# Output projection with norms out of place and stores as steps of their own, and the mixing stage's first rows beside the last attention unit

## The chip, the cores and the metric

The kernel runs on one core of one Trainium2 chip. The metric is device microseconds of one execution of the whole program. A core has five engines with an instruction queue each: TensorE (PE, with its weight loads shown as PEld), VectorE (DVE), ScalarE (ACT), GpSimd (POOL) and SyncE (SP). Here SP issues nearly all DMAs, one after the other; a DMA whose condition is not met holds everything behind it in SP's queue.

## The reference

```python
x = A_x                                               # 2048 x 576
sa, ca, ga, sb, cb, gb = silu(c) @ w_mod              # six vectors of 576
h = layernorm(x) * (1 + ca) + sa
x = x + ga * (sliding_attention(h @ wqkv) @ wo)       # 32 heads of 18, window 256
h = layernorm(x) * (1 + cb) + sb
g = gelu(layernorm(h) @ w1)                           # then four column groups shifted by +1, -1, +2, -2 rows
x1 = h + shifted(g) @ w2
x = x + gb * (x1 + gelu(layernorm(x1) @ w3) @ w4)     # w3: 576 x 4608
```

All matrix products work on operands split into a high and a low part (three products per chunk of 128), 14 matmuls for a contraction of 576.

## The kernel before

The program has three stages. `phase_a` is attention and most of the output projection, `phase_b` the mixing stage (w1, the shifts, w2), `phase_c` the large MLP. The order of instructions on every engine in `phase_a` is written out by hand: each step is a pair (time, function), the time in attention units, and `play` emits the functions by rising time. The times are a plan; on the chip each engine simply works through its queue. In `phase_b` the order is the framework's.

`phase_a` runs 32 units `u` (four blocks `g` of 512 rows by eight groups `j` of four heads). A unit lasts some 20 us. For unit `u`, `pack(u)` issues twelve DMAs from SP that gather the rows of q and k from DRAM into `Q[u % 3]` and `K[u % 3]`, planned at `u - 1.6`; they can start when the last read of that buffer, three units before, is done. `scores(u)` (planned from `u - 1` to `u`) takes row maxima, `attend(u)` (from `u + 0.38`) makes the exponentials on ACT (L549), the products with V (L560, 48 matmuls), and writes `o` to the DRAM tensor `od` (L581).

From unit 22.85 on, `s4a(t)` for the row tiles t = 0 to 11 runs beside the attention, one tile each 0.72 units: two rows are loaded (`or`, the attention output, and `xr`, the input; eight slots of `s4rows`, but tile 0 has rows of its own), `or` is transposed and multiplied with `Wo` (L786), the result added into `xr` (L791), `xr` stored to `xp` (L793), normed in place on ACT (L158), scaled and shifted in place on POOL (`mod`, L801 and L802), stored to `hbd` (L803), normed in place again (`ln2`, L158) and stored to `xnd` (L807). Each store stands right behind the instruction that makes its data. A norm in place writes the row that the store before it reads, so ACT waits until that store has landed.

The last four tiles (`s4`, t = 12 to 15) need the attention output of the last unit and run in `phase_b`, which begins with the first block's rows: `stage1(t)` loads `xn` rows from `xnd` (L984) and transposes them (L98, L104) into `xnT0`; `stage2(0)` multiplies that with five chunks of w1 (L1017) and applies the gelu (L1019, which needs another ACT table). `xnT` tiles come from a ring of three buffers.

Of the kernel before, what the change touches and what calls it, by code (L numbers as in the profile page):

```python
# [53 lines left out]
class Kern:  # L54
# [133 lines left out]

    def phase_a(self):
        nc = self.nc  # L190
        sm, gp, row = self.sm, self.gp, self.row
        self.hbd = [self.dr.tile([P, D], F32, name=f"hbd{t}") for t in range(NT)]
        self.xnd = [self.dr.tile([P, D], F32, name=f"xnd{t}") for t in range(NT)]
# [5 lines left out]
        with ExitStack() as st:  # L199
            ps = self.bank  # L200
            kv = self.pool(st, "kV")
            kp = self.pool(st, "kA")
            V = [kv.tile([P, H * VA + 13], F32, name=f"V{i}") for i in range(10)]
# [316 lines left out]
            def attend(u):  # L520
# [53 lines left out]
                def on():  # L574
                    pt = abox[2]
                    rc = sm.tile([P, 4, 4], F32, tag="rc", name=f"rc{u}", bufs=2)
                    nc.vector.reciprocal(rc, pt[:, :, :, DH])
                    o = kp.tile([P, 4, 72], F32, tag="o", name=f"o{u}", bufs=2)
                    nc.vector.tensor_tensor(out=o.rearrange("p t (h d) -> p t h d", d=DH), in0=pt[:, :, :, 0:DH], in1=rc.unsqueeze(3).to_broadcast([P, 4, 4, DH]), op=ALU.mult)
                    j = u % NU  # L580
                    nc.sync.dma_start(self.od[g].rearrange("(t p) d -> p t d", p=P)[:, :, j * 72:(j + 1) * 72], o)  # L581
                e = []
                for b in range(3):
# [2 lines left out]
                        e += [(t, xs(b, h)), (t + 0.015, ex(b, h))]  # L586
                    e.append((u + self.o_x + 1 + self.o_a - 0.001 * (2 - b), av(b)))
                t = u + self.o_x + 1 + self.o_a
                return e + [(t + 0.03, cp), (t + 0.15, ot), (t + 0.165, on)]

            def modvec(v):
                acc = []

                def load(k):
                    def f():
                        if k == 0:
                            acc.append(gp.tile([P, 2 * D], F32, tag="oT", name=f"wm{v}", bufs=1))
                            acc.extend((acc[0][:, 0:D], acc[0][:, D:]))
                        kk = P if k < KC else TAIL
                        nc.scalar.dma_start(acc[1 if k == 0 else 2][:kk], self.w_mod[k * P:k * P + kk, v * D:(v + 1) * D])  # L600
                    return f

                def add(k):
                    def f():
                        w = acc[1 if k == 0 else 2]
                        kk = P if k < KC else TAIL
                        nc.gpsimd.tensor_scalar(w[:kk], w[:kk], silu[:kk, k:k + 1], 0.0, op0=ALU.mult, op1=ALU.add)
                        if k:
                            nc.gpsimd.tensor_tensor(out=acc[1][:kk], in0=acc[1][:kk], in1=w[:kk], op=ALU.add)
                    return f  # L610

                def bcast(hf):
                    def f():
                        acc.append(ps([P, 288], "tr", f"pm{v}{hf}"))
                        nc.tensor.matmul(acc[-1], ones.to_broadcast([P, P]), acc[1][:, hf * 288:(hf + 1) * 288], start=True, stop=True)

                    def e():
                        nc.vector.tensor_scalar(acc[1][:, hf * 288:(hf + 1) * 288], acc[3 + hf], 1.0 if v == 4 else 0.0, None, op0=ALU.add)
                        if hf == 1:
                            nc.sync.dma_start(self.modd[v], acc[1][0:1, :])  # L620
                    return [(0.3, f), (0.33, e)]
# [103 lines left out]
            for t in range(12):  # L725
                t0 = w1 + 0.12 + 0.72 * t
                ev += [(t0 + d, f) for d, f in self.s4a(t, kp)]
            ev += self.load_w1(w1 + 1.2, 0.56) + self.load_w2(w1 + 4.1, 0.6)
            with self.tc.manual_schedule(engines={mybir.EngineType.SP, mybir.EngineType.PE, mybir.EngineType.DVE, mybir.EngineType.Activation, mybir.EngineType.Pool}):
                play(ev)  # L730

    win = {1: (2.9, 9.25), 2: (9.7, 16.1), 3: (16.55, 22.73)}
    o_p, o_x, o_a, g_w = 1.6, 0.38, 0.18, 0.05

    def s4a(self, t, kp):
# [39 lines left out]
        def wo(hf):  # L775
            cs = slice(hf * 288, (hf + 1) * 288)

            def part(a, b):
                def f():
                    T, W = box["T"], Wo["w"]  # L780
                    if a == 0:
                        box["po"] = ps([P, 288], "mm", f"po{t}_{hf}")
                    pl = sorted(self.products(lambda k: k, lambda k: k), key=lambda p: p[0] // KC)
                    pl = [(T[:, i, :], W[:, j, cs]) for i, j in pl]
                    for n in range(a, b):
                        nc.tensor.matmul(box["po"], pl[n][0], pl[n][1], start=(n == 0), stop=(n == len(pl) - 1))  # L786
                return f

            def add():
                x = box["x"]  # L790
                nc.vector.tensor_tensor(out=x[:, cs], in0=box["po"], in1=x[:, cs], op=ALU.add)  # L791
                if hf == 1:
                    nc.sync.dma_start(self.xp[t], x)  # L793
            return [part(a, b) for a, b in ((0, 4), (4, 8), (8, 11), (11, 14))], add

        x = lambda: box["x"]
        b1, r1, n1, g1 = self.stat_steps(x, f"b{t}")
        b2, r2, n2, g2 = self.stat_steps(x, f"c{t}")

        def mod():  # L800
            nc.gpsimd.tensor_tensor(out=x(), in0=x(), in1=self.cb, op=ALU.mult)  # L801
            nc.gpsimd.tensor_tensor(out=x(), in0=x(), in1=self.sb, op=ALU.add)  # L802
            nc.sync.dma_start(self.hbd[t], x())  # L803

        def ln2():
            self.norm(x(), x(), g2())
            nc.sync.dma_start(self.xnd[t], x())  # L807
# [141 lines left out]
    def ltile(self, name):  # L949
        if name == "LNT0":  # L950
            return self.gp.tile([P, 2 * KC + 1, 512], F32R, tag="L", name=name, bufs=1)
        return self.bc.tile([P, 2 * KC + 1, 512], F32R, tag="L2", name=name, bufs=3)

    def phase_b(self, bp):
        nc = self.nc
        self.accd = [self.dr.tile([P, D], F32, name=f"accd{t}") for t in range(NT)]
        W1, W2 = self.W1, self.W2
        shifts = (1, -1, 2, -2)
        xnT, GT = {}, {}
# [19 lines left out]
        def stage1(t):  # L979
            box = {}  # L980

            def load():
                box["x"] = self.row(f"xn{t}")[:, 0:D]
                nc.sync.dma_start(box["x"], self.xnd[t])  # L984
# [7 lines left out]
            tra, trb = self.split9(lambda: box["x"], lambda: xnT[g], slice((t % 4) * P, (t % 4 + 1) * P), f"xnT{t}", ("w1" if t < 3 else "w2") if g == 0 else "t2")  # L992
            return load, begin, trb

        def stage2(g):
# [12 lines left out]
            def w1c(fc):  # L1008
                def f():
                    if fc == KC:  # L1010
                        begin()
                    Gh, Gl = GT[g]
                    L, W = xnT[g], W1[fc]
                    pg = self.bank([P, 512], "w1", f"pg{g}_{fc}")
                    pl = self.products(lambda k: L[:, k, :], lambda k: W[:, k, :])
                    for i, (a, w) in enumerate(pl):
                        nc.tensor.matmul(pg, w, a, start=(i == 0), stop=(i == len(pl) - 1))  # L1017
                    gf = bp.tile([P, 512], F32, tag="gf", name=f"gf{g}_{fc}", bufs=2)
                    nc.scalar.activation(gf, pg, AF.Gelu_apprx_tanh)  # L1019
                    cpy = nc.vector.tensor_copy  # L1020
# [87 lines left out]
        w1t, w2s = (0.0, 0.5, 1.5, 2.5), (1.0, 2.0, 3.0, 3.5)  # L1108
        for g in range(NB):
            for i in range(4):  # L1110
                ld, tr, trb = stage1(4 * g + i)
                t0 = w1t[g] - 0.45 + 0.08 * i
                ev += [(t0 - 0.25, ld), (t0, tr), (t0 + 0.005, trb)]
# [308 lines left out]
```

## Time and profile before

| | us |
|---|---|
| three runs | 1730.81, 1737.53, 1741.58 |
| median | 1737.53 |
| the profiled execution, its own time | 1739.16 |
| its span in the profile | 1737.4 |
| PE busy in the span | 1665.6 |

In the rows of the profile a line such as `L158` is a line of the program; `SPq` and `ACTq` are DMA issues in the queue of SP and ACT; a bracket such as `[3.60 <-ACT P L549]` is idle time of the engine ahead of the row and what ended it. The rows of `windows` give, for each stretch, its length, the busy time of PE, PEld, DVE, ACT and POOL with the number of instructions, the clock that TensorE was granted as a share of full speed, the share of DMA time, and GB/s. A chain of waits on the page follows the work that ended last back through the program.

### The profile page before, as it was taken

The numbers are of one execution on the slowest core, as the hardware profiler recorded it, in microseconds if no ns is written. First come the engines' busy times: TensorE is split into PE (matmuls) and PEld (weight loads), VectorE is DVE, ScalarE is ACT, GpSimd is POOL, SyncE is SP. The second block draws the span as 40 slices with busy tenths as digits, with TensorE's granted clock in tenths as the row PEclk, the third lists the DMA queues.
The fourth block names the chain that finished last, engine by engine and source line by source line (L and its number), as shares of the span: only waits on it lengthen the run. The fifth ranks groups of instructions, "written<-read, shape, count | busy, mean of one in ns | idle before, by whom it ended". The sixth has DMA issues, their size and how long they took to land.

```text
span 1737.4 us, 30750 instructions
## 1 busy us (share of the span) xinstructions
PE 1665.6 (96%) x11100; PEld 1439.1 (83%) x11100; DVE 1172.6 (67%) x2543; ACT 700.9 (40%) x1310; POOL 812.6 (47%) x799
## 2 busy tenths in 40 slices
PE   7899999999999889999999999999999999999997
PEld 5777777877777777788989999999998999999997
DVE  3465566665567574777778888888876666666667
ACT  3254464554455555443243444343422222222221
POOL 6433141332225453044178888888864333332335
PEclk9999999999999899999999999999999999999999
DMA  5735544534557563653456555556665554445441
GB/s 167 201 122 150 150 128 134 155 107 125 137 154 197 154 195 110 203 158 103 162 182 219 210 201 187 186 206 221 216 217 166 168 165 146 143 137 168 156 150 68
DMA packets 161279, 283.33 MB, mean 163 GB/s; under 512 B 38500, under 2 KB 77412, under 8 KB 161128
## 3 DMA queue, kind: packets, MB, share of 16 engines
q1 hardware_dynamic: 158184, 275.54, 50.8%
q10 hardware_dynamic: 2944, 5.83, 1.2%
q8 instruction: 88, 1.44, 0.4%
q14 instruction: 63, 0.52, 0.1%
HBM read 168.86 MB, written 111.78 MB: 162 GB/s over the span
## 4 chain that ended last, share of the span: by engine, by line
PE 81%; DMA 6%; DVE 5%; POOL 3%; ACT 2%; issue 1%; SPq 1%; ACTq 0%; POOLq 0%; DVEq 0%
PE pall L1283 26%; PE pall L1329 22%; PE pall L391 8%; PE pall L560 4%; PE pall L530 4%; PE pall L483 4%; PE pall L1017 3%; PE pall L539 3%; PE pall L1068 2%; PE pall L786 2%; DVE pall L490 1%; DMA Q<-ms 1%; DMA wm<-in_w_mod_dram 1%; PE pall L276 1%; PE pall L571 1%
## 5 line engine op out<-in xcount | busy, mean ns | idle before, releaser
L1283 PE MATMUL pall<-LNT,W 128*128 128x512 f32 x2016 | 498.5, 390 | 1.9 <-ACT g L1287 1.9
L1329 PEld LDWEIGHTS pall<-W,G 128*128 128x128 f32 x3036 | 430.0, 189 | 25.9 <-DVE G L1249 4.3
L1329 PE MATMUL pall<-W,G 128*128 128x288 f32 x3036 | 443.4, 295 | 5.7 <-DVE G L1249 3.6
L1283 PEld LDWEIGHTS pall<-LNT,W 128*128 128x128 f32 x2016 | 365.7, 188 | 61.6 <-ACT g L1287 2.2
L490 DVE CUSTOM_DVE_ANT_0 pall<-pall,mask 128x384 f32<-128x384 f32 (+2 forms) x512 | 271.0, 543 | 209.2 <-PE pall L483 205.8
L1338 DVE TENSOR_TENSOR accA<-pall,accA 128x576 f32<-128x576 f32 x336 | 254.2, 757 | 127.3 <-PE pall L1329 115.2
L1254 POOL TENSOR_TENSOR g<-g,g 128x512 f32<-128x512 f32 x140 | 183.9, 1314 | 293.5 <-DVE G L1249 151.1
L549 ACT ACTIVATE P<-pall 128x512 f32<-128x512 f32 (+2 forms) x384 | 215.3, 570 | 166.0 <-PE pall L539 149.5
L1246 ACT CAST G<-g 128x512 fp32r<-128x512 f32 x249 | 151.0, 620 | 282.0 <-POOL g L1254 280.3
L1249 DVE TENSOR_TENSOR G<-g,G 128x512 fp32r<-128x512 f32 x249 | 241.5, 971 | 4.1 <-ACT G L1246 4.1
L483 PE MATMUL pall<-K,Q 108*128 108x384 f32 (+2 forms) x512 | 188.4, 379 | 13.5 <-DMA xnd<-s4rows 4.0
L530 PE MATMUL pall<-Q,K 110*128 110x384 f32 (+1 forms) x704 | 156.8, 297 | 16.7 <-ACT P L549 12.4
L1287 ACT ACTIVATE g<-pall 128x512 f32<-128x512 f32 x144 | 85.8, 596 | 201.7 <-PE pall L1283 192.1
L391 PE MATMUL pall<-hT,Wc 128*128 128x512 f32 x504 | 159.2, 415 | 3.4 <-ACT V L454 1.9
L1338 DVE TENSOR_TENSOR accB<-pall,accB 128x576 f32<-128x576 f32 x134 | 101.4, 757 | 89.8 <-PE pall L1329 87.7
L530 PEld LDWEIGHTS pall<-Q,K 110*128 110x128 f32 x704 | 125.1, 192 | 39.1 <-ACT P L549 20.9
L416 POOL CAST qe<-qe 128x512 fp32r<-128x512 f32 x36 | 22.6, 627 | 240.8 <-ACT qe L412 230.4
L539 PE MATMUL pall<-maskb,identb 128*128 128x256 bf16 (+1 forms) x640 | 121.4, 255 | 0.0
L483 PEld LDWEIGHTS pall<-K,Q 108*128 108x128 f32 x512 | 97.5, 195 | 21.4 <-issue 8.8
L391 PEld LDWEIGHTS pall<-hT,Wc 128*128 128x128 f32 x504 | 86.1, 192 | 17.3 <-issue 3.9
L391 PE MATMUL pall<-Wv,hT 128*128 128x288 f32 x448 | 85.0, 313 | 3.5 <-POOL Wv L334 2.4
L560 PE MATMUL pall<-P,V 128*32 128x384 f32 (+2 forms) x1408 | 86.9, 394 | 0.0
(651 smaller groups left out, 2076.9 us busy)
## 6 DMA issues: line engine op xcount, KB each, us to landing
w4d<-W SPq DMA_DIRECT2D x55, 576.0 KB
W<-w4d SPq DMA_DIRECT2D x55, 576.0 KB
w3d<-W SPq DMA_DIRECT2D x36, 640.0 KB
W<-w3d SPq DMA_DIRECT2D x36, 640.0 KB
K<-k0d SPq DMA_DIRECT2D x96, 108.0 KB
r<-in_B_w_dram SPq DMA_DIRECT2D x36, 288.0 KB
Q<-q0d SPq DMA_DIRECT2D x128, 72.0 KB
K<-k1d SPq DMA_DIRECT2D x48, 108.0 KB
```

The lines of the kernel that those rows point to most:

```text
L391: nc.tensor.matmul(pm, pl()[i][0], pl()[i][1], start=(i == 0), stop=(i == 13))
L483: nc.tensor.matmul(sc[:, lo:], q[0:2 * R3, h, i * P:(i + 1) * P], k[0:2 * R3, h // 2, i * P + lo:(i + 3) * P], start=True, stop=True)
L490: nc.vector.tensor_tensor_reduce(out=sc[:, lo:], in0=sc[:, lo:], in1=mask[:, lo:], scale=1.0, scalar=-3e38, op0=ALU.add, op1=ALU.max, accu ...
L530: nc.tensor.matmul(x[:, p0 * P:(p0 + w) * P], k[0:2 * R3 + 2, h // 2, (kb + 2) * P:(kb + 3) * P], q[0:2 * R3 + 2, h, q0 * P:(q0 + w) * P], ...
L539: nc.tensor.matmul(x[:, p0 * P:(p0 + w) * P], self.identb, m, start=False, stop=(n == len(ms) - 1))
L549: nc.scalar.activation(pt[:, c0:c1, h % 2, :], x[:, c0 * P:c1 * P].rearrange("p (a b) -> p a b", b=P), AF.Exp, scale=SCALE)
L560: nc.tensor.matmul(abox[0][32 * h:32 * h + 32, q0 * P:(q0 + w) * P], v[:, hh * VA:hh * VA + 32], Pt[b, h // 2][:, p0:p0 + w, h % 2, :], st ...
L1249: nc.vector.tensor_tensor(out=sp[m][:, 1], in0=src(), in1=sp[m][:, 0].bitcast(F32), op=sub)
L1254: nc.gpsimd.tensor_tensor(out=g[o] if o in g else gt(o), in0=g[a], in1=g[b], op=op)
L1283: nc.tensor.matmul(box["p"], box["l"][i][1], box["l"][i][0], start=(i == 0), stop=(i == 13))
L1329: nc.tensor.matmul(po, a, b, start=(n == 0), stop=(n == len(seq) - 1))
L1338: nc.vector.tensor_tensor(out=acc2[m, i], in0=po, in1=acc2[m, i], op=ALU.add)
```

## The change

It has three parts.

1. In `s4a` the first norm and `mod` write the `or` row instead of `xr`, and the second norm writes `xr` from `or`. The three stores become steps of their own: `xp` from 0.775 to 0.88, `hbd` from 1.14 (behind `mod`) to 1.46, `xnd` from 1.62 to 1.86. The norms move from 1.08 to 1.13 and from 1.62 to 1.73, `mod` from 1.14 to 1.19.
2. The store of `o` to `od` becomes a step 0.105 units behind the one that makes `o` (0.005 in the last unit), and that of a modulation vector 0.03 units behind its last addition. The input norms of blocks 1 to 3 move by 0.02 to 0.06 units behind their statistics.
3. The third buffers of Q and K are now parts of one tile `big`, which serves afterwards as `xnT0`. The loads of `xn0` to `xn4` are planned at units 30.13 to 30.53, the transposes of `xn0` to `xn3` from unit 31.1, and three of the five w1 products of the first block (chunks 4, 0, 1) between units 31.9 and 32.9, beside the last unit's attention. `big` also takes the place of the third buffer in the ring of `xnT`.

```diff
-            Q = [kv.tile([P, 4, 512], F32R, name=f"Q{i}") for i in range(3)]
-            K = [kv.tile([P, 2, 768], F32R, name=f"K{i}") for i in range(3)]
+            Q = [kv.tile([P, 4, 512], F32R, name=f"Q{i}") for i in range(2)]
+            K = [kv.tile([P, 2, 768], F32R, name=f"K{i}") for i in range(2)]
+            Q.append(big[:, 0:2048].rearrange("p (a b) -> p a b", a=4))
+            K.append(big[:, 2048:3584].rearrange("p (a b) -> p a b", a=2))
...
-                    d = (0.0, 0.03, 0.12, 0.16)
+                    d = (0.0, 0.03, 0.14, 0.22)
...
-                return e + [(t + 0.03, cp), (t + 0.15, ot), (t + 0.165, on)]
+                return e + [(t + 0.03, cp), (t + 0.15, ot), (t + 0.165, on), (t + (0.27 if u < NB * NU - 1 else 0.17), store)]
...
+            for t in range(5):
+                ev += [(w1 + 7.4 + 0.1 * t, self.xn_load(t))]
+            for t in range(4):
+                ev += self.xnt0(t, NB * NU - 0.9 + 0.2 * t)
+            for fc, t in ((KC, -0.1), (0, 0.2), (1, 0.565)):
+                ev += spread(self.w1_parts(0, fc), NB * NU + t, NB * NU + t + 0.3)
...
+        return [(t0, tr), (t0 + 0.06, hi), (t0 + 0.1, lo), (t0 + 0.07, trt), (t0 + 0.13, hit), (t0 + 0.16, lot)]
...
         def mod():
-            nc.gpsimd.tensor_tensor(out=x(), in0=x(), in1=self.cb, op=ALU.mult)
-            nc.gpsimd.tensor_tensor(out=x(), in0=x(), in1=self.sb, op=ALU.add)
-            nc.sync.dma_start(self.hbd[t], x())
-
-        def ln2():
-            self.norm(x(), x(), g2())
-            nc.sync.dma_start(self.xnd[t], x())
+            nc.gpsimd.tensor_tensor(out=y(), in0=y(), in1=self.cb, op=ALU.mult)
+            nc.gpsimd.tensor_tensor(out=y(), in0=y(), in1=self.sb, op=ALU.add)
+
+        def keep(d, r):
+            return lambda: nc.sync.dma_start(d[t], r())
...
-        e += [(0.86, b1), (0.89, r1), (1.06, n1), (1.08, lambda: self.norm(x(), x(), g1())), (1.14, mod)]
-        e += [(1.42, b2), (1.45, r2), (1.6, n2), (1.62, ln2)]
+        e += [(0.86, b1), (0.88, keep(self.xp, x)), (0.89, r1), (1.06, n1), (1.13, lambda: self.norm(y(), x(), g1())), (1.19, mod)]
+        e += [(1.46, keep(self.hbd, y)), (1.46, b2), (1.49, r2), (1.66, n2), (1.73, lambda: self.norm(x(), y(), g2())), (1.86, keep(self.xnd, x))]
...
+        if next(self.lc) % 3 == 0:
+            return self.big.rearrange("p (k n) -> p k n", k=2 * KC + 1)
+        return self.bc.tile([P, 2 * KC + 1, 512], F32R, tag="L2", name=name, bufs=2)
```

How that moves instructions is shown at three places, by the queue of one engine in each.

SP, ahead of the twelve loads of unit 28 (into Q1 and K1; the first of them is the last row). `hbd2` is the store of tile 2's modulated row, `xp3`, `xnd2` and so on likewise; `W13r` is a chunk of w1. Before:

```order
L793 DMA xp3_116<-s4rows_5434 128x576
L743 DMA s4rows_5434<-od1_130 128x576
L807 DMA xnd2_99<-s4rows_5434 128x576
L747 DMA s4rows_5434<-in_A_x_dram 128x576
L803 DMA hbd3_84<-s4rows_5434 128x576
L882 DMA W13r_6274<-in_B_w1_dram 128x4x128
L116 DMA W13r_6274<-in_B_w1_dram 64x128
L117 DMA W13r_6274<-in_B_w1_dram 64x128
L467 DMA Q1_170<-q0d3_143 18x2x512
```

Now:

```order
L811 DMA s4rows_5432<-od1_130 128x576
L871 DMA xp3_116<-s4rows_5432 128x576
L815 DMA s4rows_5432<-in_A_x_dram 128x576
L871 DMA xnd2_99<-s4rows_5432 128x576
L946 DMA W13r_6270<-in_B_w1_dram 128x4x128
L116 DMA W13r_6270<-in_B_w1_dram 64x128
L117 DMA W13r_6270<-in_B_w1_dram 64x128
L471 DMA Q1_171<-q0d3_143 18x2x512
```

The store `hbd3`, which waits for POOL, stood ahead of the loads and now stands behind the twelve of them; the loads of rows stand ahead of the stores that they followed.

SP, ahead of the twelve loads of unit 31 (again into Q1 and K1). Before:

```order
L807 DMA xnd6_103<-s4rows_5434 128x576
L747 DMA s4rows_5434<-in_A_x_dram 128x576
L984 DMA xn0_7869<-xnd0_97 128x576
L803 DMA hbd7_88<-s4rows_5434 128x576
L984 DMA xn1_7871<-xnd1_98 128x576
L984 DMA xn2_7873<-xnd2_99 128x576
L984 DMA xn3_7875<-xnd3_100 128x576
L984 DMA xn4_7914<-xnd4_101 128x576
L984 DMA xn5_7916<-xnd5_102 128x576
L793 DMA xp8_121<-s4rows_5434 128x576
L467 DMA Q1_170<-q0d3_143 18x2x512
```

Now:

```order
L815 DMA s4rows_5432<-in_A_x_dram 128x576
L871 DMA xnd6_103<-s4rows_5432 128x576
L871 DMA hbd7_88<-s4rows_5432 128x576
L471 DMA Q1_171<-q0d3_143 18x2x512
```

The six loads of `xn` rows and the store `xp8` went behind the loads of unit 31; two stores still stand right ahead of them.

PE, from the end of the last unit (`avs31` is its attention output, `or12` the row of the first tile that needs it). Before:

```order
L98 MATMUL pall_69<-ident_72,xn3_7875 128x128 x4
L571 MATMUL pall_69<-ident_72,avs31_7718 128x128 x4
...
L1017 MATMUL pall_69<-xnT0_7877,W14_5680 128x512 x9
L104 MATMUL pall_69<-ident_72,xn4_7914 64x128
L1017 MATMUL pall_69<-xnT0_7877,W10_5829 128x512 x9
L98 MATMUL pall_69<-ident_72,or12_7922 128x128 x4
```

Now:

```order
L791 MATMUL pall_69<-big_159,W11_5977 128x512 x6
L575 MATMUL pall_69<-ident_72,avs31_7792 128x128 x4
L791 MATMUL pall_69<-big_159,W11_5977 128x512 x8
L98 MATMUL pall_69<-ident_72,xn4_7372 128x128 x4
L104 MATMUL pall_69<-ident_72,xn4_7372 64x128
L98 MATMUL pall_69<-ident_72,xn5_7956 128x128 x4
L791 MATMUL pall_69<-big_159,W12_6131 128x512 x6
L104 MATMUL pall_69<-ident_72,xn5_7956 64x128
L791 MATMUL pall_69<-big_159,W12_6131 128x512 x5
L98 MATMUL pall_69<-ident_72,or12_7962 128x128 x4
```

Two and a half chunks of w1 have gone ahead of `avs31`; 19 products are left between it and `or12`.

More of the change, by code (lines that the diff above doesn't have):

```diff
@@ L579, in on, with store @@
                     nc.vector.tensor_tensor(out=o.rearrange("p t (h d) -> p t h d", d=DH), in0=pt[:, :, :, 0:DH], in1=rc.unsqueeze(3).to_broadcast([P, 4, 4, DH]), op=ALU.mult)
-                    j = u % NU
+                    abox.append(o)
+                def store():
+                    j, o = u % NU, abox[3]
                     nc.sync.dma_start(self.od[g].rearrange("(t p) d -> p t d", p=P)[:, :, j * 72:(j + 1) * 72], o)
@@ L730, in phase_a, with xn_load, f, xnt0 @@
                 play(ev)
+    def xn_load(self, t):
+        def f():
+            self.xnr[t] = self.row(f"xn{t}")[:, 0:D]
+            self.nc.sync.dma_start(self.xnr[t], self.xnd[t])
+        return f
+    def xnt0(self, t, t0):
+        nc = self.nc
+        cs = slice(t * P, (t + 1) * P)
+        box = {}
+        def tr():
+            if t == 0:
+                self.xnT[0] = self.ltile("xnT0")
+            box["p"] = self.bank([P, KC, P], "w1", f"xnT{t}pa")
+            for k in range(KC):
+                nc.tensor.transpose(box["p"][:, k, :], self.xnr[t][:, k * P:(k + 1) * P], self.ident)
+        def hi():
+            nc.scalar.copy(self.xnT[0][:, 0:KC, cs], box["p"])
+        def lo():
+            L = self.xnT[0]
+            nc.vector.tensor_tensor(out=L[:, KC:2 * KC, cs], in0=box["p"], in1=L[:, 0:KC, cs].bitcast(F32), op=ALU.subtract)
+        def trt():
+            box["q"] = self.bank([TAIL, P], "w1", f"xnT{t}pb")
+            nc.tensor.transpose(box["q"], self.xnr[t][:, KC * P:D], self.ident)
+        def hit():
+            nc.scalar.copy(self.xnT[0][:TAIL, 2 * KC, cs], box["q"])
+        def lot():
+            L = self.xnT[0]
+            nc.vector.tensor_tensor(out=L[TAIL:, 2 * KC, cs], in0=box["q"], in1=L[:TAIL, 2 * KC, cs].bitcast(F32), op=ALU.subtract)
+        return [(t0, tr), (t0 + 0.06, hi), (t0 + 0.1, lo), (t0 + 0.07, trt), (t0 + 0.13, hit), (t0 + 0.16, lot)]
+    def w1_parts(self, g, fc, n=7):
+        def part(a, b):
+            def f():
+                L, W = self.xnT[g], self.W1[fc]
+                if a == 0:
+                    self.pg[g, fc] = self.bank([P, 512], "w1", f"pg{g}_{fc}")
+                pl = self.products(lambda k: L[:, k, :], lambda k: W[:, k, :])
+                for i in range(a, b):
+                    self.nc.tensor.matmul(self.pg[g, fc], pl[i][1], pl[i][0], start=(i == 0), stop=(i == 13))
+            return f
+        e = [14 * i // n for i in range(n + 1)]
+        return [part(a, b) for a, b in zip(e, e[1:])]
+    def setup_b(self):
+        self.xnr, self.xnT, self.pg = {}, {}, {}
+        self.lc = itertools.count()
     win = {1: (2.9, 9.25), 2: (9.7, 16.1), 3: (16.55, 22.73)}
@@ L956, in phase_b @@
         self.accd = [self.dr.tile([P, D], F32, name=f"accd{t}") for t in range(NT)]
-        W1, W2 = self.W1, self.W2
+        W2 = self.W2
         shifts = (1, -1, 2, -2)
-        xnT, GT = {}, {}
+        xnT, GT = self.xnT, {}
         W2t = bp.tile([P, D], F32R, name="W2t")
@@ L982, in load @@
             def load():
-                box["x"] = self.row(f"xn{t}")[:, 0:D]
-                nc.sync.dma_start(box["x"], self.xnd[t])
+                if t not in self.xnr:
+                    self.xn_load(t)()
+                box["x"] = self.xnr[t]
             g = t // 4
@@ L1012, in f @@
                     Gh, Gl = GT[g]
[L1013 to L1017, printed above, removed]
+                    if (g, fc) not in self.pg:
+                        self.w1_parts(g, fc, 1)[0]()
+                    pg = self.pg[g, fc]
                     gf = bp.tile([P, 512], F32, tag="gf", name=f"gf{g}_{fc}", bufs=2)
```

19 lines of the change are left out of this document (10 added, 9 removed).

## The prediction

> **What bounds the kernel now.** The page first: is one engine full, and does the chain of waits run through it?
>
> ```profile
> span 1737.4 us, 30750 instructions
> PE 1665.6 (96%) x11100; PEld 1439.1 (83%) x11100; DVE 1172.6 (67%) x2543; ACT 700.9 (40%) x1310; POOL 812.6 (47%) x799
> PE 81%; DMA 6%; DVE 5%; POOL 3%; ACT 2%; issue 1%; SPq 1%; ACTq 0%; POOLq 0%; DVEq 0%
> ```
>
> TensorE is busy 96% of the span and carries 81% of the chain. The change takes no matmul away, so it can only win where TensorE stands still (1737.4 - 1665.6 = 71.8 us) or runs at a lowered clock. So the second view is the table of windows, cut at the stages: attention alone up to 480, attention beside the output projection up to 685, the step into the mixing stage up to 707.
>
> ```profile
> core 0: us, PE busy (x) PEld busy (x) DVE busy (x) ACT busy (x) POOL busy (x), PEclk, DMA share, GB/s
> 60.00:480.00 420.00, 402.95 (x3176) 324.24 (x3177) 255.97 (x894) 210.47 (x394) 118.28 (x137) 0.98 0.49 138
> 480.00:580.00 100.00, 93.01 (x806) 75.96 (x804) 70.98 (x242) 56.37 (x105) 43.91 (x53) 1.00 0.67 174
> 580.00:600.00 20.00, 14.37 (x94) 11.47 (x95) 9.21 (x33) 9.66 (x18) 11.89 (x13) 0.74 0.50 156
> 600.00:640.00 40.00, 36.61 (x327) 30.08 (x323) 29.22 (x102) 22.32 (x41) 19.77 (x26) 1.00 0.70 191
> 640.00:660.00 20.00, 15.78 (x127) 13.56 (x120) 12.11 (x43) 10.33 (x18) 6.83 (x9) 0.91 0.70 198
> 685.00:707.00 22.00, 17.02 (x127) 11.55 (x125) 8.54 (x23) 15.09 (x30) 3.60 (x4) 1.00 0.58 172
> ```
>
> I count as lost the idle time plus the busy time times the missing clock. 580 to 600: 5.63 + 14.37 x 0.26 = 9.4 us. 640 to 660: 4.22 + 15.78 x 0.09 = 5.6 us. The rest of the projection's stretch (480 to 580 and 600 to 640) loses 6.99 + 3.39 = 10.4 us in small pieces, the step into the mixing stage 4.98 us. These four are what the change can reach; behind 707 it alters little.
>
> **The change part by part.** *Norms out of place, stores later.* The first large hole, in the timelines of SP, ACT and PE:
>
> ```profile
> 562.55 0.42 SPq L747 DMA_DIRECT2D s4rows<-in_A_x_dram  x1
> 568.37 0.32 SPq L803 DMA_DIRECT2D hbd<-s4rows  x1
> 570.52 0.46 SPq L467 DMA_DIRECT2D Q<-q0d  x1
> 575.90 0.32 SPq L469 DMA_DIRECT2D K<-k1d  x1
> 576.32 0.34 SPq L793 DMA_DIRECT2D xp<-s4rows  x1
> 576.85 1.21 PE L786 MATMUL pall<-Wo,oT 128*128 128x288 f32 x8
> 582.41 0.87 ACT L158 ACTIVATE s4rows<-s4rows,b4rs 128x576 f32<-128x576 f32 x1 [4.94 <-DMA xp<-s4rows]
> 583.81 0.79 PE L530 MATMUL pall<-Q,K 110*128 110x384 f32 x2 [3.60 <-ACT P L549]
> 585.07 2.12 PE L786 MATMUL pall<-Wo,oT 128*128 128x288 f32 x8
> ```
>
> SP issues nothing from 562.97 to 568.37: `hbd3` waits for POOL. Only then come the twelve loads of unit 28 and, behind them, the store `xp4`. ACT waits 4.94 us for that store to land, because its norm writes the row that the store reads; the exponentials of the running unit are queued behind the norm, and TensorE waits 3.60 us for one. Then the clock drops: eight products of 288 columns take 2.12 us where they took 1.21.
>
> Afterwards the first norm waits for no store, and `hbd3` stands behind the loads of unit 28, so both causes go together. If only ACT's wait went, the loads would be next: the last is issued at 575.90 and lands, at the 6 us that `xp4` took from 576.32 to 582.4, near 582, little earlier than ACT came free. With `hbd3` out of the way they can go 5 us earlier. I take the 9.4 us as gone; ends: 1 us (loads late still) and 9.4.
>
> The second hole:
>
> ```profile
> 629.64 0.44 SPq L984 DMA_DIRECT2D xn<-xnd  x1
> 635.15 0.32 SPq L803 DMA_DIRECT2D hbd<-s4rows  x1
> 635.52 2.35 SPq L984 DMA_DIRECT2D xn<-xnd  x5
> 638.44 0.30 SPq L467 DMA_DIRECT2D Q<-q0d  x1
> 647.83 0.27 SPq L469 DMA_DIRECT2D K<-k1d  x1
> 653.24 0.41 PE L483 MATMUL pall<-K,Q 108*128 108x384 f32 x1 [4.02 <-DMA xnd<-s4rows]
> ```
>
> The wait is put down to a store, but the instruction is the first score of unit 31, which reads Q and K, and the last load of that unit went out at 647.83, 5.4 us before. Its twelve loads need 9.4 us from first to last issue, against 5.4 us at 570.52, because five `xn` loads of 295 KB stand right ahead of them, and all that behind a store that held SP for 5.1 us. The change moves the `xn` loads and `xp8` behind the twelve, and `hbd7` is planned 0.27 units behind `mod`. I take 5.6 us as gone; ends 1 and 5.6, since `hbd7` is still right ahead of the loads.
>
> The small pieces, by the lists of who waited for whom on SP and PE from 480 on:
>
> ```profile
> SPq L803 <- POOL s4rows L802: 32.3, 7, 5.3
> SPq L807 <- ACT s4rows L158: 20.3, 9, 4.3
> SPq L793 <- DVE s4rows L791: 15.9, 6, 4.7
> SPq L581 <- DVE o L579: 8.0, 5, 4.6
> PE pall L530 <- ACT P L549: 6.6, 6, 3.6
> PE pall L752 <- DMA s4rows<-od: 1.3, 1, 1.3
> ```
>
> SP spends 76 us of this stretch on stores that are not ready, with loads behind them. All four kinds move back by 2 us or more (0.1 units of 20 us). How much of that reaches TensorE is small: of its waits for exponentials 6.6 - 3.6 = 3.0 us are left beside the first hole, and 1.3 us for a late row. I take 4 of the 10.4 us; ends 0 and 8. The stores and norms cost the same as before wherever they stand, 0.3 us of SP and 0.87 us of ACT each; nothing is added, and the longer hold of the `or` row ends (1.86) before its slot is loaded again (2.28 units behind the tile's start). Attention alone loses 17.05 + 402.95 x 0.02 = 25 us; later `od` stores and input norms touch part of its causes. I take 1.5 us, ends -2 (a row that waits for a later store) and 6.
>
> *The first rows and products beside the last unit.* The rows of the step:
>
> ```profile
> 694.99 0.65 PE L571 MATMUL pall<-ident,avs 128*128 128x128 f32 x4 [0.17 <-ACT avs L565]
> 697.25 0.37 SPq L581 DMA_DIRECT2D od<-o  x1
> 700.96 0.42 SPq L824 DMA_DIRECT2D or<-od  x1
> 703.10 1.28 ACT L1019 ACT_TABLE_LOAD   x1 [1.54 <-DMA sbB<-modd]
> 706.75 0.63 PE L98 MATMUL pall<-ident,or 128*128 128x128 f32 x4 [1.55 <-DMA or<-od]
> 740.35 13.12 PE L1017 MATMUL pall<-xnT,W 128*128 128x512 f32 x57
> ```
>
> A product costs 13.12 / 57 = 0.230 us. 34 of them (7.8 us) move ahead of the last unit's end, into a unit in which TensorE now waits for an exponential now and then; a part of the 4.98 us goes so, and the unit ends later by what is left of the 7.8. From there a chain that the change does not shorten sets the pace: transposes of `avs31`, its store, the load of `or12`: 706.75 - 695.64 = 11.1 us. To cover it TensorE has 19 products and ten transposes left, 19 x 0.230 + 2 x 0.65 = 5.7 us. It idles 5.4 us, about as much as the 4.98 us of now. The cover has only changed sides: I take 0, ends -4 (rows land sooner since the small w2 loads are now ahead of them) and +6.
>
> Here a price in clock speaks against the change. The 3.60 us hole above was followed by a clock of 0.74 over 20 us, 3.7 us lost; the 1.55 us hole at 706.75 by none. The new idle time is split: the third chunk's products need a bank that the first gelu frees, behind the table load, so part of the waiting lies there, and I count no drop, but the 3.7 us are in the +6. [...]
>
> *`big`.* The same bytes under another name. Each load and each later write touches the part that the old buffer held, and the last reader, unit 29, is done well before `xn0` is written. Cost 0.
>
> Sum: 9.4 + 5.6 + 4 + 1.5 + 0 = 20.5 us; I take 1.5 us back for waits that come into view when the larger ones go: 19 us. The profiled execution took 1739.16 us, so 1720.2; it lies 1.6 us over the median of the runs, 1737.53, and on that basis the time is **1718.5 us**, 1.1% less.
>
> **The rivals.** *More than that goes* (-24 to -36 us, some 1708): all four of SP's kinds of waiting stop reaching TensorE: 9.4 + 5.6 + 8 + 6, with up to 4 from the step. For it: 76 us of waiting in SP's queue. Against: TensorE's own waits name few of them.
>
> *One hole stays* (-3 to -14 us, some 1729): the loads of unit 28 or of unit 31 are late still, since `xnd2` and `hbd7` stand ahead of them; 19 less 9.4 or 5.6.
>
> *Slower:* the norms are later by up to 0.11 units, and if ACT is 3 us late, `xnd2`, `hbd4` or `hbd7` hold SP ahead of the loads of units 28, 29 and 31 as `hbd3` did. From about 4 us of such a hold TensorE stops: the 5.6 us of the second hole for each of the two units that had none (29 and 30), both old holes stay, and the step costs its 6: +17 at most, about +10, some 1748. Against: `hbd` gets 0.27 units, 5 us, where the two POOL operations need 2.9.
>
> ```profile
> L801 POOL TENSOR_TENSOR s4rows<-s4rows,cb 128x576 f32<-128x576 f32 x11 | 15.6, 1421 | 31.6 <-ACT s4rows L158 31.6
> L802 POOL TENSOR_TENSOR s4rows<-s4rows,sb 128x576 f32<-128x576 f32 x11 | 15.6, 1417 | 0.9
> ```
>
> *The rows are not there in time,* so the products do not run beside the last unit: TensorE stops at `xn0`, planned a unit (20 us) after its load. Cost up to 6 us, some 1725.
>
> **How the numbers follow.** A measurement of this kernel can tell about 1% (17.4 us, 1720.2) from no change. Chances: forecast 0.48, more 0.17, one hole stays 0.18, slower 0.12, rows late 0.05. The forecast's own spread, 1713 to 1724, lies on both sides of 1720.2, two thirds of it below: faster 0.33 + 0.17 + 0.02 = 0.52. Slower by over 1% is half of the slower rival and its worst ends: 0.07. Within 1% is the rest, 0.41. The range leaves out half of the slower rival and the far end of the one that gains more: 1705 to 1740.
>
> **What would show it.** Right: no wait of L158's successor for a DMA in ACT's list, SP's waits on the four stores under 30 us, no stretch of 20 us between 480 and 680 with a clock under 0.95, and TensorE busy over 19 us in the two that now have 14.37 and 15.78. In the step: 4 to 6 us idle between the last `avs` transposes and `or12`, in two pieces. Wrong: a hole of over 3 us ahead of a first score with its loads issued late; a clock drop at the step; or the holes gone and the time unchanged, which would mean that TensorE's busy time had hidden them.

## The result, and the profile after

Ten runs of the changed kernel have a median of 1730.32 us (1728.28 to 1735.82), ten of the kernel before 1738.16 us. The ratio is 0.9965, with a 95% interval of 0.9948 to 0.9982; a second comparison (`changed_again` below) gave 0.9952 (0.9934 to 0.9970). That is 6 to 8 us less, where 19 were forecast. Where this text gives a kernel's gain, it is worked out from such a ratio of runs; the medians can differ by up to 2 us more or less. The profiled execution took 1732.08 us, 7.1 less than that of before.

The same windows as in the prediction, from the profile of the changed kernel:

```profile
span 1730.3 us, 30744 instructions
60.00:480.00 420.00, 401.76 (x3168) 322.89 (x3167) 255.54 (x891) 209.62 (x394) 118.31 (x137) 0.98 0.49 137
480.00:580.00 100.00, 92.66 (x805) 75.83 (x803) 72.25 (x243) 58.49 (x107) 43.71 (x53) 1.00 0.69 180
580.00:600.00 20.00, 19.43 (x177) 16.48 (x175) 15.74 (x55) 12.74 (x24) 12.76 (x15) 1.00 0.75 200
600.00:640.00 40.00, 38.55 (x342) 32.33 (x342) 30.49 (x112) 25.14 (x46) 22.30 (x26) 1.00 0.70 197
640.00:660.00 20.00, 18.00 (x148) 14.46 (x147) 12.79 (x47) 9.89 (x19) 9.06 (x14) 0.91 0.52 175
685.00:707.00 22.00, 17.55 (x121) 13.36 (x114) 10.13 (x21) 11.67 (x22) 0.00 (x0) 0.92 0.56 170
```

The first hole is filled (19.43 busy where 14.37 were). From 640 to 660 the clock is still 0.91, now without a hole of over 0.7 us in it. The step into the mixing stage has a lowered clock that it did not have.

Windows at fixed times compare different work once one kernel is ahead. So here are windows cut at program points, before and then after: from 480 to the last transposes of `avs`, from there to the first transposes of `or12`, and, with the window of the last products with `Wo` left out, from there to the last product with w2.

```profile
480.00:695.30 215.30, 192.97 (x1665) 156.33 (x1664) 136.28 (x472) 120.14 (x218) 96.63 (x117) 0.97 0.60 164
695.30:706.70 11.40, 8.20 (x40) 5.78 (x37) 6.27 (x16) 6.54 (x15) 0.00 (x0) 1.00 0.84 232
...
740.10:862.10 122.00, 118.20 (x757) 107.69 (x756) 92.82 (x244) 44.53 (x91) 40.76 (x55) 1.00 0.45 143
```

```profile
480.00:688.80 208.80, 195.77 (x1704) 159.73 (x1703) 140.91 (x482) 123.28 (x225) 96.41 (x117) 0.99 0.64 176
688.80:701.10 12.30, 7.87 (x33) 5.68 (x32) 5.91 (x13) 6.87 (x12) 0.00 (x0) 0.86 0.61 175
...
730.30:853.40 123.10, 116.05 (x746) 105.64 (x745) 93.51 (x248) 43.83 (x90) 41.62 (x56) 1.00 0.47 149
```

Lost time (length less busy time times clock) by stage, before and after: 28.1 and 15.0 in the projection's stretch; 3.2 and 5.5 in the step; 0.9 and 0.6 in the window left out; 3.8 and 7.1 in the mixing stage. So the first stretch gained 13.1 us, and the two behind it gave 5.6 back. (The first stretch is 6.5 us shorter although 34 products of 0.230 us, 7.8 us, were put into it, which makes 14.3; the clock has two digits.) Attention alone lost 1.2 us more than before, against the 1.5 us of gain that the sum took. One profile each cannot settle that term: in a second profile of the changed kernel the same window loses 16.7 us, at a clock of 1.00, against 26.3 in this one.

The queue of SP ahead of unit 28 and ACT's norm `b4`, which had waited 4.94 us:

```profile
566.85 0.29 SPq L471 DMA_DIRECT2D Q<-q0d  x1
...
573.81 0.32 SPq L473 DMA_DIRECT2D K<-k1d  x1
574.23 0.34 SPq L871 DMA_DIRECT2D hbd<-s4rows  x1
575.26 0.40 SPq L871 DMA_DIRECT2D xp<-s4rows  x1
...
579.52 0.86 ACT L158 ACTIVATE s4rows<-s4rows,b4rs 128x576 f32<-128x576 f32 x1
```

The first load goes out at 566.85 (before: 570.52), the twelfth ahead of `hbd3`, and the norm begins with `xp4` only 4.3 us under way and waits for nothing. The step, with all engines:

```profile
690.03 0.37 SPq L588 DMA_DIRECT2D od<-o  x1
694.00 0.32 SPq L1030 DMA_DIRECT2D sbB<-modd  x1
694.00 1.28 ACT L1084 ACT_TABLE_LOAD   x1 [1.72 <-issue]
694.06 0.11 DVE L1071 MEMSET G<- 128x20 f32 x2 [1.21 <-DMA od<-o]
694.20 0.28 DVE L106 TENSOR_TENSOR xnT<-pall,xnT 64x128 fp32r<-64x128 f32 x1
694.54 0.65 PE L98 MATMUL pall<-ident,xn 128*128 128x128 f32 x4 [2.92 <-DVE xnT L106]
694.84 0.42 SPq L888 DMA_DIRECT2D or<-od  x1
701.11 0.63 PE L98 MATMUL pall<-ident,or 128*128 128x128 f32 x4 [0.77 <-DMA or<-od]
```

Three queues come free within 0.06 us of each other, at 694.0, four microseconds after the store of the last `o` was issued: SP's (the load of `sbB`), ACT's (the table load ahead of the first gelu) and DVE's (the memset of `G`). The row of DVE names the reason, the landing of `od<-o`; SP's list of waits names it for the load of `sbB` as well. The pool of the mixing stage lies where the attention's pool lay, and `gf`, `G`, `sbB` take the place of `o`, whose last reader is that store. TensorE stands 2.92 us for a transposed row that is queued on DVE behind the memset.

### The profile page after: what moved, and what is told of

It is laid out like the page before. It is cut to its first block, busy times and chain, and to the rows that moved or that the text cites. A ratio compares the mean times of both kernels' runs of the same rounds, so it can differ in the third digit from the quotient of the medians.

```text
span 1730.3 us, 30744 instructions
## 1 busy us (share of the span) xinstructions
PE 1662.3 (96%) x11100; PEld 1436.5 (83%) x11100; DVE 1172.3 (68%) x2543; ACT 701.3 (41%) x1310; POOL 812.8 (47%) x799
## 4 chain that ended last, share of the span: by engine, by line
PE 52%; DVE 1%; POOL 1%; issue 0%; DMA 0%; ACT 0%; POOLq 0%; DVEq 0%
PE pall L1350 26%; PE pall L1396 23%; PE pall L1133 2%; PE pall L791 2%; POOL accA L1411 1%; DVE accA L1411 0%; DVE G L1316 0%; PE pall L98 0%; DVE accA L1405 0%; DMA r<-in_B_w_dram 0%; POOL c L1243 0%; POOL x L1153 0%; POOL x L1152 0%; DVE xm L160 0%; DVE accB L1405 0%
## 5 line engine op out<-in xcount | busy, mean ns | idle before, releaser
L1350 PE MATMUL pall<-LNT,W 128*128 128x512 f32 x1512 | 375.8, 390 | 1.9 <-ACT g L1354 1.9
L1350 PEld LDWEIGHTS pall<-LNT,W 128*128 128x128 f32 x1512 | 275.1, 188 | 47.8 <-ACT g L1354 2.2
L487 PE MATMUL pall<-K,Q 108*128 108x384 f32 (+2 forms) x352 | 127.9, 377 | 9.7 <-DMA wr<-in_A_wqkv_dram 4.9
L1350 PE MATMUL pall<-big,W 128*128 128x512 f32 x504 | 126.2, 390 | 0.0
L534 PE MATMUL pall<-Q,K 110*128 110x384 f32 (+1 forms) x480 | 106.0, 294 | 9.4 <-ACT P L553 5.4
L534 PEld LDWEIGHTS pall<-Q,K 110*128 110x128 f32 x480 | 85.1, 191 | 24.5 <-ACT P L553 9.9
L1350 PEld LDWEIGHTS pall<-big,W 128*128 128x128 f32 x504 | 90.9, 188 | 14.1
```

The lines of the kernel that those rows point to most:

```text
L487: nc.tensor.matmul(sc[:, lo:], q[0:2 * R3, h, i * P:(i + 1) * P], k[0:2 * R3, h // 2, i * P + lo:(i + 3) * P], start=True, stop=True)
L534: nc.tensor.matmul(x[:, p0 * P:(p0 + w) * P], k[0:2 * R3 + 2, h // 2, (kb + 2) * P:(kb + 3) * P], q[0:2 * R3 + 2, h, q0 * P:(q0 + w) * P], ...
L1350: nc.tensor.matmul(box["p"], box["l"][i][1], box["l"][i][0], start=(i == 0), stop=(i == 13))
```

## The experiments

**The kernel before, once more**, for a second profile.

> The kernel before, once more, for a second profile. Theory A: the two holes (over 3 us each) stand at the same program points, near 584 and 653, with SP's stores ahead of the loads of units 28 and 31. Theory B: one of them or both are missing or under 1 us.

One run, 1743.81 us. The two holes in its timeline of TensorE:

```profile
588.62 0.79 PE L530 MATMUL pall<-Q,K 110*128 110x384 f32 x2 [3.41 <-ACT P L549]
657.94 0.41 PE L483 MATMUL pall<-K,Q 108*128 108x384 f32 x1 [3.67 <-DMA xnd<-s4rows]
```

They belong to the program (3.60 and 4.02 us in the first profile). Theory B falls.

**Parts 1 and 2 alone**: the hunks of `s4a`, `attend`, `modvec` and the input norms, on the kernel before.

> Parts 1 and 2 of the change alone (norms out of place, stores as later steps); the mixing stage's first rows and products stay where they were before. Theory A (both holes of the projection stretch go, and the step into the mixing stage gives part of the gain back): no idle stretch of TensorE over 3 us between 560 and 660, the step as before (about 5 us idle), so 12 to 16 us less than before. Theory B (the holes come and go from execution to execution, and the one profile of before overstated them): 3 to 7 us less. Theory C (part 3 brings what there is): within 2 us of before.

1727.16 us beside 1739.6, ratio 0.9935 (0.9919 to 0.9951): 11.3 us less, a little under the 12 to 16 of theory A, and more than the 6 to 8 of the whole change (the intervals just overlap). Its stretch from 480 to the last `avs`, and its step:

```profile
480.00:680.20 200.20, 186.51 (x1650) 151.34 (x1649) 135.01 (x467) 118.81 (x215) 95.58 (x116) 0.99 0.63 174
680.20:692.50 12.30, 8.30 (x40) 5.87 (x38) 7.06 (x17) 7.40 (x16) 0.00 (x0) 1.00 0.82 234
```

15.6 us lost, as in the changed kernel (15.0); 4.0 in the step, at full clock. Of the six `xn` loads one stands ahead of unit 31's loads here and one among them, and the second hole is gone too.

**Part 3 alone**: the changed kernel with the same hunks taken back.

> Part 3 alone (first transposed rows and 42 products in the fixed buffer beside the last unit); norms in place and stores as before. Theory A: the first hole near 584 stays, the second near 650 goes or shrinks because the xn loads are out of the way (-4 to -6 us), and the step costs 3 to 5 us more than before, with a lowered clock: -2 to +2 us. Theory B: -1 to +1. Theory C: 5 to 8 us less.

1743.66 us beside 1739.6, ratio 1.0013 (0.9995 to 1.0031), 2.3 us more, just over theory A's upper end of 2. In its timeline of TensorE the first hole stands as before (ACT's norm waits 4.63 us for `xp`), the second is down to 1.1 us, and the step has its hole and a clock of 0.85:

```profile
587.57 0.50 PE L534 MATMUL pall<-big 110*128 110x384 f32 x2 [3.26 <-ACT P L553]
708.93 0.66 PE L98 MATMUL pall<-ident,xn 128*128 128x128 f32 x4 [2.56 <-DVE xnT L106]
```

**The products back behind the unit:**

```diff
-            for fc, t in ((KC, -0.1), (0, 0.2), (1, 0.565)):
-                ev += spread(self.w1_parts(0, fc), NB * NU + t, NB * NU + t + 0.3)
```

> The changed kernel, except that the first block's five chunks of w1 products all stay in the mixing stage; its transposed rows are still made beside the last unit. Theory A (the products that moved ahead of the last unit are missing as cover while the last attention output goes through DRAM): the idle time between the last avs transposes and the or12 transposes falls from 4.4 to under 2 us and no clock drop follows, so 3 to 5 us less than the changed kernel, 10 to 12 less than before. Rival (the chain sets the end whatever covers it, or the bank of the first gelu does): the same as the changed kernel within 1 us.

1724.95 us beside 1739.6, ratio 0.9921 (0.9908 to 0.9934), 13.7 us less. The time is what theory A expected and more, the reason only in part: 3.3 us of idle time are left in the step, not under 2, but at full clock, and the mixing stage behind `Wo` is back at 4.4 us.

```profile
683.90:696.00 12.10, 8.79 (x45) 6.51 (x43) 6.17 (x13) 6.99 (x12) 0.00 (x0) 1.00 0.76 219
```

**The last `o` in a buffer of its own**, in the changed kernel:

```diff
-                    o = kp.tile([P, 4, 72], F32, tag="o", name=f"o{u}", bufs=2)
+                    o = kp.tile([P, 4, 72], F32, tag="o", name=f"o{u}", bufs=2) if u < NB * NU - 1 else self.sm.tile([P, 4, 72], F32, tag="o31", name=f"o{u}", bufs=1)
```

> The changed kernel with the last unit's o in a buffer that the mixing stage's pool does not reuse, so that the first gelu and the memset of G no longer wait for the store of that o to land. Theory D (in the step, ACT and DVE stand still until that store has landed, 4 us, because their output buffers lie where o lay; that, not the missing cover alone, makes the 2.92 us hole and the clock drop behind it): the table load starts right behind the avs copy, no hole over 2 us before the or12 transposes, no clock drop there, 1.5 to 3.5 us less than the changed kernel (8 to 10 less than before). Rival E (TensorE has only some 6 us of work between the last avs transposes and or12, wherever the gelu stands): the idle time stays at 4 to 5 us in other pieces, the time within 1 us of the changed kernel.

1723.33 us beside 1738.79, ratio 0.9901 (0.9883 to 0.9918): 17.2 us less than before (15.5 between the medians). The wait is gone as theory D expected, with a longest hole of 1.54 us ahead of `or12`, but its "no clock drop" failed: a stretch at half rate of 3.41 us begins at 694.25, right behind that hole. The gain is more than theory D expected, so the kernel was run again beside the changed kernel itself:

> The changed kernel again, beside the three others of this call on the same chip. Both theories: 5 to 9 us less than before; the hole of nearly 3 us ahead of a transposed row in the step and a clock drop behind it, as in its first profile.

> o31_elsewhere again, beside the changed kernel. Theory D (the wait for the landing of the last o is what the step costs): 4 to 8 us less than changed_again. Rival (half of the difference between the two earlier calls was the chip): 1 to 3 us less.

Changed kernel 1730.66 us, ratio 0.9952 (0.9934 to 0.9970); `o31_again` 1723.95 us, 0.9922 (0.9900 to 0.9944); before 1738.51 us. The two ratios differ by 0.0030, 5.2 us, though their intervals overlap a little. The changed kernel's step in this second profile, in its window and the row of its hole, and behind it that of `o31_again`, with the rows of ACT, SP and TensorE:

```profile
682.20:694.30 12.10, 8.48 (x33) 6.05 (x31) 5.81 (x13) 6.86 (x12) 0.00 (x0) 0.76 0.54 174
687.83 0.66 PE L98 MATMUL pall<-ident,xn 128*128 128x128 f32 x4 [2.87 <-DVE xnT L106]
```

```profile
685.90:695.30 9.40, 7.77 (x40) 6.00 (x39) 6.66 (x14) 8.25 (x14) 0.00 (x0) 1.00 0.72 196
686.33 0.32 SPq L1030 DMA_DIRECT2D sbB<-modd  x1
686.33 1.28 ACT L1084 ACT_TABLE_LOAD   x1 [1.44 <-PE pall L575]
687.22 0.38 SPq L588 DMA_DIRECT2D od<-o  x1
692.27 0.32 SPq L888 DMA_DIRECT2D or<-od  x1
695.31 0.63 PE L98 MATMUL pall<-ident,or 128*128 128x128 f32 x4 [1.40 <-DMA or<-od]
```

Table load and `sbB` now go ahead of the store, the step loses 1.6 us instead of 12.1 - 8.48 x 0.76 = 5.7, and no hole is longer than 1.4. Two things changed at once. The gelu frees its bank early, so that 27 products run in the step where the changed kernel had 19 (counted in the traces). And the first transposes of `or12` begin 3.0 us after the issue of its load, where it took 6.3 in the first profile of the changed kernel, with the loads of `sbB` and `cbB` right ahead of it there. That holds in every profile: 2.9 to 3.0 us in the five with the last `o` moved, 5.5 to 6.9 in the nine others, which have these two loads right ahead. Moving `o` does both, and the shares were not told apart. Rival E, that TensorE has only some 6 us of work there whatever the gelu does, falls.

**Both remedies, and the remedy without part 3:** the last `o` in its own buffer with all products behind the unit, with parts 1 and 2 alone, and with two chunks beside the unit, `((KC, -0.1), (0, 0.2))`.

> The changed kernel with all of the first block's products behind the last unit and the last o in a buffer of its own; the load of sbB then stands ahead of the store of o, not between it and the load of or12. Theory D and the cover together: TensorE idles under 1.5 us between the last avs transposes and or12 (3.34 us in products_behind_unit), 1 to 3 us less than products_behind_unit, 15 to 17 less than before. Rival: the load of or12 sets the pace as before, within 1 us of products_behind_unit.

> norms_stores_only with the last o in a buffer of its own: the same release, without the rows and products beside the last unit. If part 3 is worth something once that wait is gone, this is 2 to 4 us slower than o31_again. Rival (the rows and products beside the last unit bring nothing of their own): within 1 us of o31_again, 14 to 16 us less than before.

> o31_elsewhere with two of the three chunks beside the last unit, the third behind it, as cover for the load of or12. If the cover still counts: the idle time ahead of or12 falls from 1.75 us to under 1, and 0.5 to 1.5 us less than o31_again. Rival (it doesn't, the first gelu keeps the banks free): the same within 1 us.

Ratios 0.9910 (0.9890 to 0.9930), 0.9929 (0.9908 to 0.9950) and 0.9936 (0.9917 to 0.9955). The first is 1.9 us better than `products_behind_unit`, the second 1.2 us worse than `o31_again`, the third 2.4 us worse, all inside the intervals. The first still idles 2.8 us ahead of `or12`, not under 1.5. The second lies between its two expectations, with 12.3 us less than before: once the wait is gone, the rows and products beside the last unit have no gain of their own that these measurements can see. It shows another thing too: without part 3, the last `o` in its own buffer is worth 1.0 us (0.9935 and 0.9929, from two comparisons), with part 3 it is worth 5 us and more. The third kernel's expectation of more cover failed: it idles 3.2 us ahead of `or12`, more than `o31_again`.

**The two halves of part 1, apart**, both on `norms_stores_only`. Norms out of place, all steps at their old times:

```diff
-... (0.88, keep(self.xp, x)), ... (1.13, lambda: self.norm(y(), x(), g1())), (1.19, mod)]
-... (1.46, keep(self.hbd, y)), ... (1.73, lambda: self.norm(x(), y(), g2())), (1.86, keep(self.xnd, x))]
+... (0.776, keep(self.xp, x)), ... (1.08, lambda: self.norm(y(), x(), g1())), (1.14, mod)]
+... (1.141, keep(self.hbd, y)), ... (1.62, lambda: self.norm(x(), y(), g2())), (1.621, keep(self.xnd, x))]
```

> As norms_stores_only, but with the three stores, the norms and mod at their old times: only the out-of-place norms are left of part 1. The prediction's step (with ACT's wait gone, the late loads of unit 28 are next): a hole of TensorE of 2 us or more stays near 584 with hbd3 still ahead of the loads, and the time is 3 to 7 us less than before. Rival (the wait for the landing in ACT was the whole hole): no hole over 1 us near 584, 9 to 12 us less.

And the stores later, all in place:

```diff
-        x, y = lambda: box["x"], lambda: box["o"]
+        x = y = lambda: box["x"]
```

> As norms_stores_only, but with the norms and mod in place: only the later stores are left. Theory A (ACT's norm waits for the landing of the store of the row that it writes): xp4 now stands behind the loads of unit 28 and hbd3, so ACT waits for it 3 us or more, TensorE has a hole of 2 us or more between 575 and 600, and the time is 3 to 7 us less than before. Rival (the queue of SP was the whole cause): no such hole, 9 to 12 us less.

Out of place alone: 1736.71 us, ratio 0.9982 (0.9969 to 0.9995), 3.1 us less. Later stores alone: 1743.49 us, 1.0021 (1.0000 to 1.0041), 3.7 us more. Both together: 11.3 less. Part 2 is in all three kernels and was not run alone. In the first, the loads of unit 28 are late still, and near 584 a hole of 1.29 us is left, between the 2 us of the one expectation and the 1 us of the other (SP and PE):

```profile
572.01 0.32 SPq L807 DMA_DIRECT2D hbd<-s4rows  x1
574.17 0.45 SPq L467 DMA_DIRECT2D Q<-q0d  x1
585.56 0.41 PE L483 MATMUL pall<-K,Q 108*128 108x384 f32 x1 [1.29 <-DVE mr L496]
594.15 0.50 PE L530 MATMUL pall<-Q,K 110*128 110x384 f32 x2 [2.03 <-ACT P L549]
```

The last row is no part of the first hole. It stands in the kernel before as well, 11 us behind the first hole, and the 5.63 us of idle time from 580 to 600 are the two together, 3.60 + 2.03 (before; ACT and PE):

```profile
593.62 0.87 ACT L158 ACTIVATE s4rows<-s4rows,c4rs 128x576 f32<-128x576 f32 x1 [1.45 <-DVE c4rs L143]
595.02 0.50 PE L530 MATMUL pall<-Q,K 110*128 110x384 f32 x2 [2.03 <-ACT P L549]
```

ACT waits there for the statistics of the second norm, with the exponentials queued behind. This hole stands in all four profiles in which the norms keep their old times (both of before, part 3 alone, this kernel) and in none of the ten in which they stand later, so it goes with the later steps, not with the rows out of place. Norms and stores moved together in all of the ten; that it is the norms' part is read from ACT's queue and was not run apart.

In the second kernel the holes moved rather than stayed: there is none near 584, but two where ACT's norm waits for the row that a later `xp` store reads (SP, ACT, PE; the trace puts the first wait down to a load of long before, but the norm reads and writes the row that the store of 533.96 reads):

```profile
533.96 0.67 SPq L807 DMA_DIRECT2D xp<-s4rows  x1
540.46 0.87 ACT L158 ACTIVATE s4rows<-s4rows,b1rs 128x576 f32<-128x576 f32 x1 [7.31 <-DMA s4rows<-in_A_x_dram]
542.58 0.80 PE L530 MATMUL pall<-Q,K 110*128 110x384 f32 x2 [5.53 <-ACT P L549]
644.14 0.87 ACT L158 ACTIVATE s4rows<-s4rows,b8rs 128x576 f32<-128x576 f32 x1 [5.40 <-DMA xp<-s4rows]
645.54 0.80 PE L530 MATMUL pall<-Q,K 110*128 110x384 f32 x2 [4.06 <-ACT P L549]
```

## Why the prediction was right and wrong

**Right: the two holes and their causes.** Both are there in both profiles of before and gone in the changed kernel. That the remedies for SP's order and ACT's wait belong together is shown by the halves of part 1, which bring -3.1 and +3.7 us apart and -11.3 together. The window of the first hole gave 8.8 of the 9.4 us that the prediction took. In part that was luck: 2.03 us of its idle time had another cause, ACT's second norm ahead of its statistics, which the prediction did not see and which went with the later steps. The slower rival, loads held up as `hbd3` held them, did not come; the change without its out-of-place norms was the one that ended on that side.

**Too large: the rest of the projection's stretch.** This is the larger share of what is missing from the 19 us, and a matter of size. For the stretch and attention alone the sum had 20.5 us (9.4 + 5.6 + 4 + 1.5), less the 1.5 taken back; parts 1 and 2 alone brought 11.3. In the first profile the lost time fell by 13.1 less 1.2. The window from 640 to 660 still loses 2.0 + 18.00 x 0.09 = 3.6 us of its 5.6, and the small pieces fell from 10.4 to 7.3 + 1.5 = 8.8 us, by 1.6 where 4 were taken; why so few of them went was not tested and stays open. The 1.6 us of clock in the window from 640 to 660 had no hole of over 0.7 us ahead of it and did not return: in the second profile no stretch is lowered between 405 and 688, and the projection's stretch loses 13.4 us. "SP's waits on the four stores under 30 us" was wrong as well, and would have been a poor sign: they are 58 us now by the same four rows (76 before), but the loads stand ahead of the stores.

**Wrong: "The cover has only changed sides: I take 0".** This is the step whose mechanism failed: part 3 made the kernel some 3 to 5 us slower than parts 1 and 2 alone, where 0 was taken. In the first profile step and mixing stage gave 5.6 us back (2.3 and 3.3). Two things were wrong in it.

The sum set 5.4 us of idle time between `avs31` and `or12` beside "the 4.98 us of now", but those 4.98 are of the window from 685 to 707, which begins 10 us ahead of the last transposes of `avs`. Between the same two points the kernel before idles 3.2 us, so the prediction's own figure meant a loss of some 2 us. The step measured 4.4 us idle (its sign "4 to 6 us idle" came true) and 1.1 us of clock: 5.5 against 3.2.

And the prediction saw that the third chunk needs a bank that the first gelu frees, but put the delay down to the table load of 1.28 us. The gelu in fact waits for the landing of the last `o`, 4 us behind its issue (690.03 and 694.00 above). In the kernel before that wait did not show (DVE and PE; the store was issued at 697.25):

```profile
700.19 0.11 DVE L1004 MEMSET G<- 128x20 f32 x2 [0.19 <-DMA od<-o]
700.69 2.33 PE L1017 MATMUL pall<-xnT,W 128*128 128x512 f32 x9
```

The store had landed by 700.2, and the nine products are the last of chunk 4, which the first gelu reads: they end at 703.02, and the table load begins at 703.10. The change put chunk 4 ahead of the last unit's end, so that the gelu had nothing left to wait for but the store. Of the two remedies one puts the cover back (13.7 us less than before) and one removes the wait (13.6 and 17.2): the step then loses 3.3 and 1.6 us in place of 5.5. And without part 3 removing the wait is worth 1.0 us. These three together are why the cause counts as shown; how much of the second remedy is the earlier gelu and how much the quicker load of `or12` stays open. "I count no drop" was wrong too: the clock fell in the step in both profiles of the changed kernel, and in that of part 3 alone (0.86, 0.76 and 0.85).

**Wrong: "behind 707 it alters little".** The mixing stage lost 3.3 us more, in two holes, of which the trace shows the first so (ACT, DVE, PE):

```profile
743.88 0.87 ACT L158 ACTIVATE xr<-xr,c15rs 128x576 f32<-128x576 f32 x1 [4.31 <-DVE c15rs L143]
745.91 0.69 DVE L1088 TENSOR_TENSOR G<-gf,G 128x512 fp32r<-128x512 f32 x1 [2.07 <-ACT G L1087]
747.10 1.85 PE L1133 MATMUL pall<-W,G 128*128 128x288 f32 x12 [1.65 <-DVE x L1134]
```

The last row's norm stands ahead of the last gelu on ACT, and TensorE has 47 products between `Wo` and w2 where it had 57, so it is there 2.3 us sooner relative to that chain and waits. `products_behind_unit` has 59 products there, not this hole, and 4.4 us lost in the stage. With the last `o` moved 50 products stand there and this hole is gone, but another of 1.7 us follows and the stage still loses 5.9 us; what of the 3.3 us is due to the order alone stays open.

The forecast's direction and the range held; the forecast of 19 us did not, and neither did the reasons of the rival nearest in time ("one hole stays", 1729): no hole stayed, the gain was spent elsewhere. The sum by stages, -13.1 + 2.3 - 0.3 + 3.3 + 1.2, makes -6.6 us of the 7.1 between the two profiled executions.

## What to carry to other kernels

A wait that costs nothing because other work lies beside it becomes a cost when that work is moved: before products are moved ahead of a join, list what every engine waits for in the join, the release of buffers to the next stage among it. A buffer whose last reader was a DMA came free here when that DMA had landed (in the changed kernel 4 us after its issue), so the last tile that a stage stores should lie outside the memory that the next stage takes over. And in-place work and the time of its store are one decision: a later store frees the queue but holds the next writer. Here the later stores alone lost 3.7 us, the norms out of place alone gained 3.1, and both together 11.3.

## What the runs showed of the hardware

The clock fell in or behind much shorter holes than the 3.60 us one that the prediction counts (in the first profile of the changed kernel, at 693.77 in the hole of 2.92 us that ends at 694.54), and not at each of them. In the clock records of the 14 profiles of this case (60 to 1650 us), the lowered stretches are at half rate (0.50) and 3.41 us long, or twice that. They began in or within 3.5 us after 13 of 14 holes of TensorE of 3 us and more, 15 of 25 of 2 to 3 us, 18 of 52 of 1.5 to 2 and 8 of 85 of 1 to 1.5; ten lowered stretches had no hole of even 0.9 us ahead of them. One stretch costs up to 1.7 us (half of 3.41), so a hole of 2 to 3 us costs, by an estimate from these counts, about 1 us more than its length on average. No length of hole divides those with a fall from those without one in these counts.
